# A fused attention and mixture-of-experts kernel: four groups of instructions are put elsewhere in the written order

## The chip, the cores and the metric

One core of a Trainium2 chip runs the whole program in one launch. The metric is the device time of one execution in microseconds (us). The kernel before takes 757.58 us, the median of 3 runs (757.49 to 758.53).

## The reference

Three layers follow each other in float32.

```python
# 1. attention, 4 batches x 8 heads, 576 positions, 64 dims; heads 0-3 see the last 32 positions,
#    heads 4-7 see the earlier positions that are congruent mod 32
attn = softmax(where(mask, q @ k.T / 8, -1e9)); x = (attn @ v) as [2304, 512]
# 2. dense layer, 512 -> 2048 -> 512
x = (s * relu(x @ w_in) ** 2 + b) @ w_out
# 3. experts: each token goes to one of 8 experts with room for 288 each, given out greedily by falling logit
logits = x @ w_gate
for (token, e) in argsort(-logits.flatten()):
    if token is free and counts[e] < 288: assigned[token] = e
out[assigned == e] = relu(x[assigned == e] @ w1[e]) @ w2[e]
```

## The kernel before

The order of all instructions is written by hand (a manual schedule): each engine executes its own instructions in the order in which the Python code emits them. The work is cut into generators, each `yield` ending one step; a `Pipe` (L46) starts a generator every so many ticks, and one `tick` advances all that are live by one step, oldest first.

Every float32 product is made of three: an operand is split into a high half (a cast on ScalarE, the engine ACT) and a low half (a subtraction on VectorE, DVE), and high x high, high x low and low x high are accumulated.

Attention (`attn_unit`, L234) has 32 units; one starts every second tick. A unit loads, makes scores (L254), takes a softmax on DVE and ACT, turns the weights by PE transposes (L292, L294), copies them, and multiplies with v (L313). For batches 0 and 1 the scores fall on even ticks and the transposes on odd ones (2 and 9 ticks after the start); for batches 2 and 3 (2 and 10 ticks) both fall on even ticks, and the older unit's transposes are emitted ahead of the newer one's scores.

`prep` (L372) decodes w_in and w_out. A slice of w_out is written to DRAM (L400), added into the column sums `acc` (L402, L404), and folded with the gate. `prep_end` (L456) multiplies `acc` with a matrix of ones and scales it by b (L459, L460). `load_out` (L449) reads the slices of w_out back later and splits them.

`mix1` (L565) interleaves attention, the first product (`h_step`, L469, 96 steps of 12 matmuls) and the preparation. The second product, x2, is done late: for each of 6 token groups and 16 slices `late_step` (L649) loads the activations r (L652), makes the high half u (L664) and the low half (L667), and puts 9 matmuls in a queue; each of these steps is one tick of `late_pipe`. `x2_late` (L685) hands the queued matmuls (L694) out one by one, and ticks the pipe when the queue is empty. After the last matmuls of a group come three calls of `x2_row` (L526), which combine an accumulator with `acc` on DVE (L530) and write 128 rows to DRAM from SP's queue (L531).

These matmuls fill PE while DVE decides the routing. `run` (L1045) takes a number from each `yield` of `route` (L740) and hands out that many x2 matmuls ("fill") before `route` goes on. A round of routing (7 in all, L805) picks each token's best open expert (`pick`, L801; L808 to L811) and finds each expert's threshold in four steps of 6 bits: a comparison with 64 candidates on DVE (L818, L820), a fill of FA0 (20) or FA (12), counting matmuls (L824), three small operations (L826 to L828), a fill of FB (7), and a matmul that spreads the result (L830). Then come T1, G1 and gsb (L831 to L834), a fill of FP (8), prefix sums (L726), a fill of FC (8), and the change of the assignment (L838 to L844), which runs straight into the next round's pick and first comparison. At the end FE gives the fills 4, 14 and 10. Every third yield `prep2` (L877) advances the loading and splitting of the first expert's weights (L367, L369).

Of the kernel before, what the change touches and what calls it, by code (L numbers as in the profile page):

```python
# [9 lines left out]
F32R = mybir.dt.float32r  # L10
# [64 lines left out]
class Body:  # L75
# [10 lines left out]
    E = 8  # L86
# [2 lines left out]
    WS = 68  # L89
    CA = 4  # L90
    LATE0 = 30
    FA0 = 20
    FA = 12
    FB = 7
    FP = 8
    FC = 8
    UB = 4
# [1 line left out]
    P1S = 28  # L99
    A2S = 8  # L100
    TM = 2
    FE = (4, 14, 10)
    P0S = 24
    AE = 2
    LOADLAG = 2
# [128 lines left out]
    def attn_unit(self, b, hp, hf):  # L234
# [51 lines left out]
        nc.vector.tensor_tensor(  # L286
            E[:pr], E[:pr], sm.unsqueeze(2).to_broadcast([pr, nb, kw]), op=ALU.mult)
        yield from self.lag(2, b)
        tps = [self.ps() for _ in range(2 if loc else 1)]
        for c in range(nb if loc else 4):  # L290
            if loc:
                nc.tensor.transpose(tps[c % 2][:96, 128 * (c // 2):128 * (c // 2) + 128], E[:, c, :], self.identf)  # L292
            else:
                nc.tensor.transpose(tps[0][:, 128 * c:128 * c + pr], Ep[:pr, 2 * c:2 * c + 2, :].rearrange("p m k -> p (m k)"),  # L294
                                    self.identf[:pr, :pr])
        yield
        eTs = []
        for t, tp in enumerate(tps):
# [20 lines left out]
        else:  # L319
            dst = self.xb[b][:, hp, :].rearrange("d (i m c) -> d m c i", m=2, c=8)[:, :, 4 * hf:4 * hf + 4]  # L320
            for m in range(2):
                (nc.vector.tensor_copy if m and self.OV else nc.scalar.copy)(
                    dst[:, m], o[m][:, :144].rearrange("d (c i) -> d c i", c=4))
        self.units += 1

    def keep_warm(self, n):
        if n:
# [44 lines left out]
    def prep(self, i):  # L372

        nc = self.nc
        fc = i // 2
        raw = self.conv_load(i)
        for _ in range(self.CA):
            yield
        rv = [t.rearrange("p (f t) -> p f t", t=2) for t in raw]
        K = self.wt([128, 512], I32, "K")  # L380
        ts = nc.vector.tensor_scalar
        half = (slice(0, 256), slice(256, 512))
        for r, h in zip(rv, half):
# [12 lines left out]
        yield  # L396
        if i % 2 == 0:
            yield from self.split(W, lambda v: self.win.__setitem__(fc, v))
            return
        nc.sync.dma_start(self.wod[fc], W)  # L400
        if fc == 0:
            nc.scalar.copy(self.acc, W)  # L402
        else:
            nc.vector.tensor_tensor(self.acc, self.acc, W, op=ALU.add)  # L404
        yield
        yield
        ps = self.ps()
        for dc in range(4):
            nc.tensor.transpose(ps[:, dc * 128:(dc + 1) * 128], W[:, dc * 128:(dc + 1) * 128], self.identf)  # L409
        yield  # L410
        WT = self.wt([128, 512], F32, "WT")
        nc.scalar.copy(WT, ps)
        yield
        self.WTs.append(WT)
        if len(self.WTs) < 4:
# [12 lines left out]
        ps = self.ps()  # L428
        for k in range(4):
            nc.tensor.transpose(ps[:, k * 128:(k + 1) * 128], go[:, k * 128:(k + 1) * 128], self.identf)  # L430
        yield
        nc.vector.tensor_reduce(self.wog[:, fc * 8 - 24:fc * 8 + 8].rearrange("p (f e) -> p f e", e=8),
                                ps.rearrange("p (f c e) -> p f e c", f=4, c=4)[:, :, :8, :], axis=AX.X, op=ALU.add)
        yield
        self.nwog += 4
        if self.nwog == 16:
            self.prep_end()

    def prep_begin(self):
        self.win, self.wout, self.xb, self.xg = {}, {}, {}, {}  # L440
        self.wod = self.dr.tile([16, 128, 512], F32, name="wod")
        self.nwog = self.units = self.ne = 0
        self.acc = self.c.tile([128, 512], F32, name="acc")
        self.wog = self.c.tile([128, 16 * 8 + 24], F32, name="wog")
        self.gate = self.c.tile([128, 4, 32], F32, name="gate")
        self.WTs = []
        self.sb = self.c.tile([128, 2], F32, name="sb")

    def load_out(self, fc):  # L449
        t = self.wt([128, 512], F32, "wo")  # L450
        self.nc.sync.dma_start(t, self.wod[fc])
        yield
        yield
        yield from self.split(t, lambda v: self.wout.__setitem__(fc, v))

    def prep_end(self):  # L456
        nc = self.nc
        ps = self.ps()
        nc.tensor.matmul(ps, self.onesf, self.acc, start=True, stop=True)  # L459
        nc.scalar.activation(self.acc, ps, AF.Copy, scale=self.sb[:, 1:2])  # L460
        ps = self.ps()
        nc.tensor.matmul(ps[:, :128], self.onesf, self.wog[:, :128], start=True, stop=True)
        lc = self.c.tile([128, 8], F32, name="lc")
        nc.vector.tensor_reduce(lc, ps[:, :128].rearrange("p (f e) -> p e f", e=8), axis=AX.X, op=ALU.add)
        nc.vector.tensor_scalar(lc, lc, self.sb[:, 1:2], None, op0=ALU.mult)
        self.lc = lc
# [52 lines left out]

    def x2_list(self, fc, acc, u, t=0):  # L520
        wh, wl = self.wout[fc]
        return [dict(out=acc[t + k], lhsT=u[:, j, k * 128:(k + 1) * 128], rhs=_alt(w),
                     start=(fc == 0 and i == 0), stop=(fc == 15 and i == 2))
                for k in range(u.shape[2] // 128) for i, (j, w) in enumerate(((0, wh), (0, wl), (1, wh)))]

    def x2_row(self, g, t, acc):  # L526
        nc = self.nc
# [37 lines left out]
    def mix1(self):  # L565
        nc = self.nc
        self.prep_begin()
        att, att2 = (Pipe(self.attention(*b), self.AE) for b in ((0, 1), (2, 3)))
        att.tick(self.AE)
        self.constants()  # L570
        self.L = self.c.tile([128, 18, 8], F32, name="L")
        self.R = self.c.tile([128, 18, 8], F32, name="R")
# [19 lines left out]
        ready = [(8, 0, dc) for dc in range(4)] + [(10, 1, 2), (11, 1, 0), (13, 1, 3), (14, 1, 1)]  # L592
        k = self.AE
        while self.units < 14 or not self.win or ready:
            att.tick()
            if k == self.SL:
                self.small_loads()
                nc.vector.memset(self.wog, 0.0)
                nc.gpsimd.iota(self.R, pattern=[[0, 18], [1, 8]], base=1, channel_multiplier=0,
                               allow_small_or_imprecise_dtypes=True)  # L600
            while ready and self.units >= ready[0][0]:
                self.group_x(*ready.pop(0)[1:])
            if self.KS <= k < self.KE:
                self.keep_warm(self.KW)
            if k >= self.P0S and k % self.P0R == 0:
                prep.tick()
            k += 1
# [3 lines left out]
        while True:  # L611
# [6 lines left out]
                if len(self.win) <= fc:  # L618
                    continue
            if self.units < 16:  # L620
                att.tick()
            elif n >= self.A2S:
                att2.tick()
            if n >= self.FS:
                for _ in range(self.FT):
                    if folds.started < len(order) and order[folds.started][1] >= self.nwog:
# [1 line left out]
                    folds.tick()  # L628
            if n >= self.WL and (n % 2 == 0 or n >= 84) and (lout.started < self.nwog or lout.started == 16):
                lout.tick()  # L630
            if n >= 95 and self.late_pipe.t < 5:
                self.late_pipe.tick()
            if fc == 12 and 0 < g < 5:
                need = 8 * (((g + 2) * self.G - 1) // self.S + 1)
                while self.units < need:
                    (att if self.units < 16 else att2).tick()
            if n == self.RC:
                self.route_consts()
            if n >= 96:
# [9 lines left out]
    def late_step(self, g, fc):  # L649
# [4 lines left out]
        yield  # L654
        last = g == self.last_late
        nt = 2 if last else 3
        u = self.p2.tile([128, 2, self.G], F32R, tag="u", name=self.nm("u"), bufs=self.UB)[:, :, :nt * 128]
        parts = [(u, r[:, :nt * 128])]
        if last:
            n = ("xh", "xl")[fc % 2]  # L660
            ul = self.xs.tile([128, self.G], F32R, tag=n, name=self.nm("ul"))[:, :256].rearrange("p (j t) -> p j t", j=2)
            parts.append((ul, r[:, 256:]))
        for d, src in parts:
            nc.scalar.copy(d[:, 0, :], src)  # L664
        yield
        for d, src in parts:
            nc.vector.tensor_tensor(d[:, 1, :], src, _f(d[:, 0, :]), op=ALU.subtract)  # L667
        yield
        if fc == 0:
            self.xacc[g] = self.x2_begin()  # L670
# [69 lines left out]
    def route(self):  # L740
# [64 lines left out]
        for rnd in range(7):  # L805
# [36 lines left out]
            tt(R, R, A1, op=ALU.mult)  # L842
            if rnd:
                tt(open_, open_, left, op=ALU.mult)  # L844
        pick()
        self.Rt, self.qt = R, q
        yield self.FE[0]
# [301 lines left out]
```

## Time and profile before

| | |
|---|---|
| time, median of 3 runs | 757.58 us |
| profiled execution, own time | 758.38 us |
| its span, first to last instruction | 756.5 us |
| PE (TensorE matmuls) busy | 731.5 us, 97% |
| PEld (weight loads) busy | 651.9 us, 86% |
| DVE, ACT busy | 497.5 us, 374.6 us |
| mean granted TensorE clock | 0.993 |

The profiled execution is one run with the hardware profiler. "Busy" counts the stretches covered by an instruction; matmuls are pipelined, so that one's end lies behind the next one's start, and the ends are modelled. Time not covered is the engine's idle time, and the profile names the instruction that ended it. By time the program has the attention start (0 to 55 us), the mix of attention and first product (to 315 us), the x2 product with the routing (to 526 us) and the experts.

### The profile page before, as it was taken

The page shows a single profiled execution, that of the slowest core. Times are in us where ns is not written, and L with a number is a line of the kernel's source. Part 1 is how long each engine was busy: PE and PEld are TensorE (multiplying, and loading weights), DVE is VectorE, ACT ScalarE, POOL GpSimd, SP SyncE. Part 2 cuts the span into 40 slices and gives each one's busy share as a digit, 9 for nine tenths or more (in the row PEclk, how much of TensorE's full clock was granted, in tenths as well). Part 3 has the DMA queues.
Part 4 walks back from the last instruction along what each step waited for, and adds up shares of the span by engine and source line. Part 5 has one row for each costly group of instructions (what it writes and reads, how often), then busy time and mean ns, then how long its engine had stood idle before and what let it go on. Part 6 is the DMA issues. An engine that isn't in the chain of part 4 may idle for free.

```text
span 756.5 us, 16924 instructions
## 1 busy us (share of the span) xinstructions
PE 731.5 (97%) x6436; PEld 651.9 (86%) x6436; DVE 497.5 (66%) x1229; ACT 374.6 (50%) x893; POOL 51.7 (7%) x69
## 2 busy tenths in 40 slices
PE   7979999999999999999989999999999999999996
PEld 5759999999999888787768887878999999999994
DVE  8789999898762133377777878687366666656620
ACT  3788776667766556422222232231355555555520
POOL 1000000000000000000000000000303221221211
PEclk9999999999999999999999999999999999999998
DMA  7885955774885799644325343342677668667411
GB/s 182 230 272 175 295 183 179 232 248 160 286 304 196 225 287 303 199 144 138 141 83 184 122 137 105 102 139 81 194 242 228 177 188 249 213 166 225 136 32 31
DMA packets 88752, 140.19 MB, mean 185 GB/s; under 512 B 10848, under 2 KB 52576, under 8 KB 88672
## 3 DMA queue, kind: packets, MB, share of 16 engines
q1 hardware_dynamic: 85600, 129.68, 54.5%
q0 software_dynamic: 3072, 9.44, 3.9%
q8 instruction: 50, 0.82, 0.5%
q14 instruction: 30, 0.25, 0.1%
HBM read 106.32 MB, written 32.77 MB: 184 GB/s over the span
## 4 chain that ended last, share of the span: by engine, by line
PE 88%; DVE 5%; DMA 4%; issue 1%; ACT 1%; SPq 0%; POOLq 0%; DVEq 0%; ACTq 0%
PE b L476 25%; PE b L694 19%; PE b L952 12%; PE b L977 11%; PE b L254 3%; DMA qk<-in_q_dram 2%; PE b L313 2%; PE b L513 2%; DMA r<-ud 1%; PE b L1015 1%; PE b L906 1%; DVE E L530 1%; PE b L993 1%; PE b L330 1%; PE b L409 1%
## 5 line engine op out<-in xcount | busy, mean ns | idle before, releaser
L694 PE MATMUL b<-wh,u 128*128 128x512 f32 x544 | 170.7, 390 | 5.5 <-DVE u L667 5.5
L694 PEld LDWEIGHTS b<-wh,u 128*128 128x128 f32 x544 | 101.5, 191 | 21.1 <-DVE u L667 7.7
L664 ACT CAST u<-r 128x384 fp32r<-128x384 f32 (+1 forms) x96 | 47.1, 493 | 141.2 <-PE b L694 102.2
L694 PE MATMUL b<-wl,u 128*128 128x512 f32 x272 | 105.6, 388 | 0.0
L977 PE MATMUL b<-u,wh 128*128 128x288 f32 x448 | 87.9, 293 | 0.0
L476 PE MATMUL b<-xh,wh 128*128 128x384 f32 x384 | 83.3, 340 | 0.0
L369 DVE TENSOR_TENSOR wl<-raw,wh 128x512 fp32r<-128x512 f32 x128 | 82.9, 683 | 0.4
L481 ACT ACTIVATE r<-b 128x384 f32<-128x384 f32 x96 | 47.0, 489 | 64.4 <-PE b L476 63.1
L476 PE MATMUL b<-xh,wl 128*128 128x384 f32 x384 | 78.9, 328 | 0.0
L476 PE MATMUL b<-xl,wh 128*128 128x384 f32 x384 | 78.8, 328 | 0.0
L367 ACT CAST wh<-raw 128x512 fp32r<-128x512 f32 x128 | 73.2, 618 | 1.5 <-DVE u L667 1.5
L952 PE MATMUL b<-X,wh 128*128 128x288 f32 x512 | 73.4, 286 | 0.6 <-ACT X L925 0.6
L476 PEld LDWEIGHTS b<-xh,wh 128*128 128x128 f32 x384 | 62.8, 190 | 8.6 <-issue 3.8
L977 PEld LDWEIGHTS b<-u,wh 128*128 128x128 f32 x448 | 69.4, 189 | 0.0
L952 PEld LDWEIGHTS b<-X,wh 128*128 128x128 f32 x512 | 67.4, 189 | 1.3 <-ACT X L925 0.7
L959 DVE SCALAR_TENSOR_TENSOR u<-b,u 128x288 fp32r<-128x288 f32 x64 | 29.2, 455 | 57.9 <-ACT u L958 43.8
L476 PEld LDWEIGHTS b<-xh,wl 128*128 128x128 f32 x384 | 65.5, 191 | 0.3 <-DVE wl L369 0.3
L476 PEld LDWEIGHTS b<-xl,wh 128*128 128x128 f32 x384 | 65.6, 191 | 0.0
L977 PE MATMUL b<-u,wl 128*128 128x288 f32 x224 | 64.1, 286 | 0.0
L694 PEld LDWEIGHTS b<-wl,u 128*128 128x128 f32 x272 | 51.8, 191 | 6.3
L667 DVE TENSOR_TENSOR u<-r,u 128x384 fp32r<-128x384 f32 (+1 forms) x96 | 49.1, 529 | 12.4 <-ACT u L664 12.3
L482 ACT ACTIVATE r<-r 128x384 f32<-128x384 f32 x96 | 50.5, 526 | 3.0
(211 smaller groups left out, 1113.5 us busy)
## 6 DMA issues: line engine op xcount, KB each, us to landing
raw<-in_moe_w_dram SPq DMA_DIRECT2D x128, 256.0 KB
r<-ud SPq DMA_DIRECT2D x160, 192.0 KB
ud<-r SPq DMA_DIRECT2D x96, 192.0 KB
raw<-in_words_dram SPq DMA_DIRECT2D x64, 256.0 KB
qk<-in_q_dram SPq DMA_DIRECT2D x24, 288.0 KB
x2d<-E SPq DMA_DIRECT2D x18, 256.0 KB
wod<-K SPq DMA_DIRECT2D x16, 256.0 KB
wo<-wod SPq DMA_DIRECT2D x16, 256.0 KB
```

The costliest lines, as they stand in the source:

```text
L254: nc.tensor.matmul(sp[64 * j:64 * j + p, c * kw:(c + 1) * kw], qk[sl, 0, q0:q0 + p], qk[sl, 1, k0:k0 + kw], start=after, stop=after or c = ...
L367: nc.scalar.copy(h, W)
L369: nc.vector.tensor_tensor(l, W, _f(h), op=ALU.subtract)
L476: nc.tensor.matmul(ps[:, :self.G], w[:, dc * 128:(dc + 1) * 128], _alt(self.xg[g][dc][x]), start=(k == 0), stop=(k == 11))
L481: nc.scalar.activation(_two(r), _nat(ps[:, :self.G]), AF.Relu)
L482: nc.scalar.activation(r, r, AF.Square)
L664: nc.scalar.copy(d[:, 0, :], src)
L667: nc.vector.tensor_tensor(d[:, 1, :], src, _f(d[:, 0, :]), op=ALU.subtract)
L694: self.nc.tensor.matmul(**args)
L952: self.nc.tensor.matmul(ps[:, :288], w1[dc, fh][wi][:, fs:fs + 128], _alt(X[:, xi, dc, :]), start=(k == 0), stop=(k == 11))
L959: self.nc.vector.scalar_tensor_tensor(_two(l), _nat(ps[:, :288]), 0.0, _two(_f(h)), op0=ALU.max, op1=ALU.subtract)
L977: nc.tensor.matmul(y[dc][:, :288], w[:, sl], _alt(u[:, j, :288]), start=(fc == 0 and i == 0), stop=(fc == 7 and i == 2))
```

## The change

Constants: FA0 20 to 13, FB 7 to 6, FE's third fill 10 to 20, and a new fill FK of 9 in rounds 0 to 5, between the change of the assignment and the next pick. In attention the transposes are collected while a tick runs and emitted at its end (`attend`). The column sums are taken from the slices that `load_out` reads back, and the product with ones follows the last of them. `late_step` waits one tick more between the low half and the matmuls; for groups 0 to 4 its halves are two tiles from a pool of 8 each, instead of one from a pool of 4.

```diff
-    FA0 = 20
+    FA0 = 13
+    FK = 9
-    FB = 7
+    FB = 6
-    FE = (4, 14, 10)
+    FE = (4, 14, 20)
...
-        tps = [self.ps() for _ in range(2 if loc else 1)]
-        for c in range(nb if loc else 4):
...
+        tps = []
+        def turn():
+            tps.extend(self.ps() for _ in range(2 if loc else 1))
+            for c in range(nb if loc else 4):
...
+        self.turns.append(turn)
         yield
...
+    def attend(self, pipe):
+        pipe.tick()
+        for turn in self.turns:
+            turn()
+        self.turns.clear()
...
         nc.sync.dma_start(self.wod[fc], W)
-        if fc == 0:
-            nc.scalar.copy(self.acc, W)
-        else:
-            nc.vector.tensor_tensor(self.acc, self.acc, W, op=ALU.add)
...
         yield from self.split(t, lambda v: self.wout.__setitem__(fc, v))
+        if fc == 0:
+            nc.scalar.copy(self.acc, t)
+        else:
+            nc.vector.tensor_tensor(self.acc, self.acc, t, op=ALU.add)
+        if fc == 15:
+            yield
+            yield
+            yield
+            ps = self.ps()
+            nc.tensor.matmul(ps, self.onesf, self.acc, start=True, stop=True)
+            nc.scalar.activation(self.acc, ps, AF.Copy, scale=self.sb[:, 1:2])
     def prep_end(self):
-        ps = self.ps()
-        nc.tensor.matmul(ps, self.onesf, self.acc, start=True, stop=True)
-        nc.scalar.activation(self.acc, ps, AF.Copy, scale=self.sb[:, 1:2])
...
-            if n >= 95 and self.late_pipe.t < 5:
+            if n >= 95 and self.late_pipe.t < 6:
...
-        u = self.p2.tile([128, 2, self.G], F32R, tag="u", name=self.nm("u"), bufs=self.UB)[:, :, :nt * 128]
+        if last:
+            u = self.p2.tile([128, 2, self.G], F32R, tag="u", name=self.nm("u"), bufs=self.UB)[:, :, :nt * 128]
+            u = u[:, 0], u[:, 1]
+        else:
+            u = [self.xs.tile([128, self.G], F32R, tag=n, name=self.nm("u")) for n in ("xh", "xl")]
...
         for d, src in parts:
-            nc.vector.tensor_tensor(d[:, 1, :], src, _f(d[:, 0, :]), op=ALU.subtract)
+            nc.vector.tensor_tensor(d[1], src, _f(d[0]), op=ALU.subtract)
+        yield
         yield
...
             tt(R, R, A1, op=ALU.mult)
             if rnd:
                 tt(open_, open_, left, op=ALU.mult)
+            if rnd < 6:
+                yield self.FK
         pick()
```

In `mix1` each tick of the attention pipes becomes a call of `attend`.

## Rows read from the trace of the kernel before

**Rows 1.** Busy time of each engine in stretches; then clock, DMA share, GB/s.
```profile
50.00:55.00 5.00, 2.47 (x36) 1.72 (x32) 4.79 (x15) 4.44 (x15) 0.00 (x0) 1.00 0.74 244
55.00:60.00 5.00, 5.00 (x33) 4.93 (x30) 4.93 (x14) 3.90 (x11) 0.00 (x0) 0.66 0.01 3
...
100.00:150.00 50.00, 50.00 (x635) 45.61 (x634) 45.58 (x110) 33.19 (x81) 0.00 (x0) 1.00 0.60 191
...
350.00:400.00 50.00, 45.43 (x289) 36.33 (x288) 36.75 (x92) 12.64 (x25) 0.00 (x0) 0.97 0.46 155
```
**Rows 2.** PE's waits, whole span: us in total, times, longest.
```profile
PE b L694 <- DVE u L667: 5.5, 4, 3.4
...
PE b L313 <- ACT eT L302: 1.8, 2, 0.9
PE b L292 <- DVE E L286: 0.8, 1, 0.8
...
PE b L830 <- DVE jc L828: 0.5, 1, 0.5
PE b L870 <- DVE rt L865: 0.3, 1, 0.3
PE b L824 <- DVE rt L820: 0.3, 1, 0.3
```
**Rows 3.** The chain of waits, 340 to 400 us: start, us, what.
```profile
381.27 1.61 PE b L694 x7
...
393.08 3.54 PE b L694 x9
...
396.87 1.85 PE b L694 x7
```
**Rows 4.** PE in order of time: start, duration, operation [idle before <-releaser].
```profile
371.76 0.39 PE L824 MATMUL b<-rt 128*128 128x16 bf16 x9
...
373.61 0.18 PE L830 MATMUL b<-J,unit 128*128 128x1 bf16 x1
...
385.36 0.46 PE L694 MATMUL b<-wl,u 128*128 128x512 f32 x1
...
389.33 0.38 PE L694 MATMUL b<-wl,u 128*128 128x512 f32 x1
393.08 0.70 PE L694 MATMUL b<-wh,u 128*128 128x512 f32 x2 [3.37 <-DVE u L667]
```
**Rows 5.** DVE in order of time, the same stage.
```profile
360.34 0.17 DVE L838 TENSOR_SCALAR rt<-b 128x8 f32<-128x8 f32 x1 [0.40 <-PE b L736]
...
361.78 0.30 DVE L802 TENSOR_REDUCE rt<-R 128x18 f32<-128x144 f32 x1
...
363.49 1.36 DVE L818 TENSOR_TENSOR rt<-rt,cand 128x1152 bf16<-128x1152 f32 x1
364.76 1.49 DVE L667 TENSOR_TENSOR u<-r,u 128x384 fp32r<-128x384 f32 x3
...
372.67 0.08 DVE L828 DVE_READ_ACCUMULATOR jc<-jo 64x1 bf16 x1
373.84 1.42 DVE L820 SCALAR_TENSOR_TENSOR rt<-rt,b,cand 128x1152 bf16<-128x1152 f32 x1 [1.09 <-PE b L830]
...
386.08 1.41 DVE L530 SCALAR_TENSOR_TENSOR E<-b,sb,acc 128x512 f32<-128x512 f32 x2 [1.48 <-PE b L694]
```
**Rows 6.** By line: the operations on the column sums.
```profile
L404 DVE TENSOR_TENSOR acc<-acc,K x15: 674/685/696, 152.1 to 231.8; 128x512 f32<-128x512 f32 x15
L460 ACT ACTIVATE acc<-b,sb x1: 687/687/687, 251.9 to 251.9; 128x512 f32<-128x512 f32 x1
```
**Rows 7.** ACT in order of time, at the start of the x2 product.
```profile
314.14 1.32 ACT L664 CAST u<-r 128x384 fp32r<-128x384 f32 x3
```
**Rows 8.** Waits of DVE, whole span, and of SP's queue, 313 to 526 us.
```profile
DVE u L667 <- ACT u L664: 12.3, 2, 11.9
...
SPq L531 <- DVE E L530: 97.2, 13, 23.6
```

More of the change, by code (lines that the diff above doesn't have):

```diff
@@ L288, in attn_unit @@
         yield from self.lag(2, b)
-        tps = [self.ps() for _ in range(2 if loc else 1)]
-        for c in range(nb if loc else 4):
-            if loc:
-                nc.tensor.transpose(tps[c % 2][:96, 128 * (c // 2):128 * (c // 2) + 128], E[:, c, :], self.identf)
-            else:
-                nc.tensor.transpose(tps[0][:, 128 * c:128 * c + pr], Ep[:pr, 2 * c:2 * c + 2, :].rearrange("p m k -> p (m k)"),
-                                    self.identf[:pr, :pr])
+        tps = []
+        def turn():
+            tps.extend(self.ps() for _ in range(2 if loc else 1))
+            for c in range(nb if loc else 4):
+                if loc:
+                    nc.tensor.transpose(tps[c % 2][:96, 128 * (c // 2):128 * (c // 2) + 128], E[:, c, :], self.identf)
+                else:
+                    nc.tensor.transpose(tps[0][:, 128 * c:128 * c + pr],
+                                        Ep[:pr, 2 * c:2 * c + 2, :].rearrange("p m k -> p (m k)"), self.identf[:pr, :pr])
+        self.turns.append(turn)
         yield
@@ L400, in prep @@
         nc.sync.dma_start(self.wod[fc], W)
-        if fc == 0:
-            nc.scalar.copy(self.acc, W)
-        else:
-            nc.vector.tensor_tensor(self.acc, self.acc, W, op=ALU.add)
         yield
@@ L440, in prep_begin @@
         self.win, self.wout, self.xb, self.xg = {}, {}, {}, {}
+        self.turns = []
         self.wod = self.dr.tile([16, 128, 512], F32, name="wod")
@@ L449, in load_out @@
     def load_out(self, fc):
+        nc = self.nc
         t = self.wt([128, 512], F32, "wo")
-        self.nc.sync.dma_start(t, self.wod[fc])
+        nc.sync.dma_start(t, self.wod[fc])
         yield
@@ L521, in x2_list @@
         wh, wl = self.wout[fc]
-        return [dict(out=acc[t + k], lhsT=u[:, j, k * 128:(k + 1) * 128], rhs=_alt(w),
+        return [dict(out=acc[t + k], lhsT=u[j][:, k * 128:(k + 1) * 128], rhs=_alt(w),
                      start=(fc == 0 and i == 0), stop=(fc == 15 and i == 2))
-                for k in range(u.shape[2] // 128) for i, (j, w) in enumerate(((0, wh), (0, wl), (1, wh)))]
+                for k in range(u[0].shape[1] // 128) for i, (j, w) in enumerate(((0, wh), (0, wl), (1, wh)))]
     def x2_row(self, g, t, acc):
@@ L568, in mix1 @@
         att, att2 = (Pipe(self.attention(*b), self.AE) for b in ((0, 1), (2, 3)))
-        att.tick(self.AE)
+        for _ in range(self.AE):
+            self.attend(att)
         self.constants()
@@ L594, in mix1 @@
         while self.units < 14 or not self.win or ready:
-            att.tick()
+            self.attend(att)
             if k == self.SL:
@@ L620, in mix1 @@
             if self.units < 16:
-                att.tick()
+                self.attend(att)
             elif n >= self.A2S:
-                att2.tick()
+                self.attend(att2)
             if n >= self.FS:
@@ L635, in mix1 @@
                 while self.units < need:
-                    (att if self.units < 16 else att2).tick()
+                    self.attend(att if self.units < 16 else att2)
             if n == self.RC:
@@ L656, in late_step @@
         nt = 2 if last else 3
-        u = self.p2.tile([128, 2, self.G], F32R, tag="u", name=self.nm("u"), bufs=self.UB)[:, :, :nt * 128]
+        if last:
+            u = self.p2.tile([128, 2, self.G], F32R, tag="u", name=self.nm("u"), bufs=self.UB)[:, :, :nt * 128]
+            u = u[:, 0], u[:, 1]
+        else:
+            u = [self.xs.tile([128, self.G], F32R, tag=n, name=self.nm("u")) for n in ("xh", "xl")]
         parts = [(u, r[:, :nt * 128])]
@@ L660, in late_step @@
             n = ("xh", "xl")[fc % 2]
-            ul = self.xs.tile([128, self.G], F32R, tag=n, name=self.nm("ul"))[:, :256].rearrange("p (j t) -> p j t", j=2)
+            ul = self.xs.tile([128, self.G], F32R, tag=n, name=self.nm("ul"))
+            ul = ul[:, :128], ul[:, 128:256]
             parts.append((ul, r[:, 256:]))
         for d, src in parts:
-            nc.scalar.copy(d[:, 0, :], src)
+            nc.scalar.copy(d[0], src)
         yield
         for d, src in parts:
-            nc.vector.tensor_tensor(d[:, 1, :], src, _f(d[:, 0, :]), op=ALU.subtract)
+            nc.vector.tensor_tensor(d[1], src, _f(d[0]), op=ALU.subtract)
+        yield
         yield
```

## The prediction

> **What bounds the kernel now.** I read the busy time by stretches first, then PE's waits, then the order of time on PE and DVE where PE waits longest. PE is the bound: from 100 to 150 us it has no idle time, though DVE is 91% busy and ACT 66% beside it [rows 1]. An edit can then only give back time in which PE waits or runs slowly. That time lies in two places. One is the end of the first half of attention (50 to 55 us, PE busy 2.47 of 5 us [rows 1]). The other is the x2 product with the routing (315 to 526 us), where 350 to 400 us alone has 4.57 us idle at a mean clock of 0.97 [rows 1].
>
> In the second place PE waits 5.5 us, four times, for a low half (L667), and 0.5, 0.3 and 0.3 us for the routing's own operations [rows 2]. The longest wait shows how. DVE runs a round's change of the assignment straight into the next pick and first comparison: start at 360.34, pick at 361.78, comparison at 363.49, and only then, at 364.76, three low halves [rows 5]. That is 4.4 us without a low half, while a low half is emitted one tick, 9 matmuls, ahead of its own matmuls. In the next round two calls of x2_row stood ahead of the same chunk (386.08, 1.41 us [rows 5]) and a third behind it; PE ran out at 389.5 and waited 3.37 us [rows 4]. The chain then has 9 matmuls in 3.54 us and 7 in 1.85, where 7 take 1.61 otherwise [rows 3]: the granted clock had fallen to the lower of its two levels, 1.2 instead of 2.4 GHz.
>
> At one point a rule of the notes says more. The Trainium skill ("Trainium Kernel Development and Optimization", Performance Expectations) holds matmul busy time for a poor measure, since matmuls are pipelined, and weight-load busy time for a good one. By weight loads 350 to 400 us is only 36.33 of 50 us busy [rows 1], so 13.7 us would be free instead of 4.57, and up to 9 us more could be won there. The fill itself says no: 19 of its matmuls start between 385.36 and 389.33 [rows 4], 0.22 us apart, against 0.213 us for 512 columns at 2.4 GHz. I go by PE's idle time.
>
> **Part by part.** *Transposes behind scores: 0.* For batches 0 and 1 the two never share a tick, so PE's order stays. For batches 2 and 3 it is reversed, in a stretch where PE has no idle time [rows 1] and waits for neither a softmax nor a weight copy: all such waits of the trace (1.8 and 0.8 us [rows 2]) are those of 50 to 55 us, before that half starts. What is queued behind scores that wait for a load would now include the transposes. Bounds: -0.3 to +0.5 us. It follows that the first place stays as it is.
>
> *Column sums: +0.2.* 15 additions of 0.685 us [rows 6], 10.3 us of DVE, leave 152 to 232 us and come after the slices are read back (241 to 303 us), where DVE waits for loads. PE is busy in both, so neither end counts. The product with ones and its scaling (0.687 us on ACT [rows 6]) move from 251 us to the step before the first x2 matmul. There ACT makes the first high halves at 314.14 [rows 7], directly ahead of PE's need at 314.9. With 0.7 us more in its queue and some 0.9 us more of PE ahead, ACT comes about 1.1 us later against 0.9 for PE. Between 0 and 0.7, I take 0.2.
>
> *The low halves' extra tick, 8 buffers, the split round: -5.5, and the clock -1.8.* The tick puts 18 matmuls (4.0 us) instead of 9 between a low half and its use. The fill of 9 lets one through between the pieces of 1.44 us (360.34 to 361.78) and 1.71 + 1.36 = 3.07 us [rows 5]. Neither piece reaches 4.0 us, so the four waits of 5.5 us go. With the 3.4 us gap the slow stretch after it goes: 3.54 - 9 x 0.23 = 1.5, and 1.85 - 1.61 = 0.24, in all about 1.8 us [rows 3]. The larger pool lets ACT make high halves sooner; DVE waits for one only twice in the whole trace, 11.9 of 12.3 us in one wait ahead of the first of them [rows 8], so 0 for that.
>
> *FA0 20 to 13, FB 7 to 6, FK 9: +3.7, -1.1.* A round has 13 + 3 x 12 + 4 x 6 + 8 + 8 + 9 = 98 matmuls instead of 100. From the prefix sums to the counting matmuls there are now 8 + 9 + 13 = 30, 6.6 us. DVE needs 0.24 + 1.44 + 0.5 (one low half) + 3.07 = 5.25 us; 1.35 us are spare. From the counting matmuls (371.76 [rows 4]) DVE's three operations are done at 372.75 [rows 5], and L830 followed at 373.61 [rows 4]; one matmul less leaves 0.6 of the 0.86 us. An ordinary round has no wait.
>
> Rounds with rows of x2 do. One row is 0.7 us on DVE and cannot start before PE has made its accumulator. The rows lie behind matmuls 138, 141 and 144 of each group's 144. The mix hands out 13 x 3 = 39, the fills before round 0 are 30 + 4 + 3 + 12 = 49, so round r starts at 88 + 98r, with the parts of a round at 13, 19, 31, 37, 49, 55, 67, 73, 81, 89 and 98. (Before, 39 + 49 + 700 + 28 = 816, all that the queue has.)
>
> - Group 0: 50, 53, 56 of round 0, behind counting work: 0.
> - Group 1: 96 of round 1 falls between the pieces, the other two behind the comparison. The row waits for PE until 3.5 us after the prefix sums and ends at 4.2; plus 3.07 is 7.3 against 6.6: 0.7 us. Then two rows, a low half and the three operations (1.4 + 0.5 + 0.56) end at 9.7, where L830 was due at 7.3 + 0.25 + 6 x 0.22 = 8.9: 0.8 us.
> - Group 2: 44, 47, 50 of round 3: two rows behind one comparison, one ahead of the next with an L369: 0.3 us.
> - Group 3: all three at 90, 93, 96 of round 4. They end at 4.3, a low half at 4.8, plus 3.07 is 7.85 against 6.6: 1.2 us.
> - Group 4: 38, 41, 44 of round 6, behind a comparison that ends at 1.65: with 2.1 of rows, 0.6 of low halves and 0.56, done at 4.85 where L830 was due at 4.2: 0.65 us.
>
> Together 0.7 + 0.8 + 0.3 + 1.2 + 0.65, some 3.7 us. Lower bound 0.5, if rows start earlier than their accumulators suggest; upper bound 6, if each of the six changes costs another 0.4. Before, rows fell elsewhere and cost, beside the waits for low halves, the 0.5 and 0.3 us that go now.
>
> SP's queue: a write of rows waits there for DVE (97.2 us in 13 waits [rows 8]), and the loads of r stand behind it. The extra tick emits one more load ahead of it. From load to low half is as before, three ticks, 27 matmuls or 6 us: 0.
>
> *FE 10 to 20:* 34 fills instead of 24 cover DVE's chain ahead of L870, so its 0.3 us go. Handed out in the route are 39 + 49 + 6 x 98 + 89 + 38 = 803; the last 13 run after L870, ahead of the 48 matmuls that cover the first gather. The last row is as much later as those 48: 0.
>
> **The sum.** Removed 5.5 + 1.8 + 0.5 + 0.3 + 0.3 = 8.4; new 3.7 + 0.2 = 3.9; net -4.5 us. The profiled execution took 758.38 us, 756.5 of span and 1.9 around it, and would take 753.9. The median is 0.8 lower, so 753.1 us. The forecast's own range is 751.1 to 754.6.
>
> **Rivals.** *All waits go:* DVE reaches the rows with time to spare, as the spare 1.35 us of ordinary rounds and 13 us of DVE idle in 350 to 400 us [rows 1] speak for. Against it: rows block everything queued behind them. 757.6 - 8.2 = about 749.6 us.
>
> *The lower clock stays:* group 1 has two waits 2 us apart, 1.5 us together, group 3 one of 1.2. At 50 to 55 us waits of at most 0.9 us each sufficed: PE was busy 2.47 of 5 us and the clock of 55 to 60 us is 0.66 [rows 1]. Against it: 1.5 us is less than 2.53. Price 1.8 us, once or twice: 754.9 to 756.7 us. The Trainium skill ("TensorE: Matmul & The Clock Gate", Why this matters for your kernels) asks that PE have no long gaps between bursts; by it short separate waits would cost no clock and 753.1 would stand, but the stretch from 50 to 60 us differs.
>
> *The waits only change their name:* the row, not the low half, holds DVE, and PE stands at L824 or L830 for as long as before. 757.6 - 1 to + 1: about 757 us.
>
> *Slower:* the 13 matmuls ahead of L824 (2.9 us) are fewer than its piece of DVE takes (3.07). If DVE comes late to the change in every round, behind low halves that wait for r behind SP's queue, the fill of 9 is no cover. It decides once DVE is 1.35 us late; at 2.8 us late, six rounds cost 6 x 1.45 = 8.7 us, above the 8.4 removed, and with one slow stretch the time is about 759.5 us. Against it: behind the first low half, DVE is held by a high half for 0.4 us in all [rows 8].
>
> **How the numbers follow.** The forecast has 0.50, all waits gone 0.13, the lower clock 0.14, renamed waits 0.13, slower 0.10. A change within 0.2% (1.5 us) is about what a measurement of this kernel can't tell from none. The clock rival lies on the faster side almost wholly, the renamed one on no change. Faster 0.76, same 0.14, slower 0.10. The range of 749.4 to 757.0 leaves out the slower case, half of the renamed waits and a small end of the best case.
>
> **What would show it.** After: no wait of PE for L667 above 1 us, the clock at 1.00 throughout 315 to 526 us, and PE's waits there at L824 and L830 next to rows of x2, some 3.9 us in all. 50 to 60 us as before. Another long wait for a low half, waits at L824 in rounds without rows, or a gain in the attention stretch would make the working wrong.

## The result and the profile after

The changed kernel takes 751.53 us, the median of 4 runs (750.04 to 752.22). Before, on the same chip, it was 757.54 us (757.26 to 758.53, 4 runs). The ratio is 0.9916, with a 95% interval of 0.9896 to 0.9935: 0.8% faster, inside the range of 749.4 to 757.0 and 1.6 us below the forecast of 753.1. The profiled execution took 752.19 us, 749.8 of span.

The stretches of [rows 1], in the changed kernel (us; busy time of PE, PEld, DVE, ACT, POOL; clock, DMA share, GB/s):

```profile
50.00:55.00 5.00, 4.20 (x42) 3.42 (x43) 4.86 (x15) 4.36 (x14) 0.00 (x0) 0.54 0.31 116
55.00:60.00 5.00, 5.00 (x28) 4.78 (x28) 4.86 (x14) 4.11 (x13) 0.00 (x0) 0.77 0.00 0
100.00:150.00 50.00, 48.63 (x652) 45.29 (x651) 46.11 (x111) 33.74 (x80) 0.00 (x0) 1.00 0.62 200
350.00:400.00 50.00, 48.83 (x328) 39.82 (x325) 40.13 (x105) 17.28 (x35) 0.00 (x0) 1.00 0.57 190
```

From 350 to 400 us PE has 1.17 us idle, where it had 4.57, and its clock is full. That was forecast. From 100 to 150 us PE now has 1.37 us idle, where it had none. That was not. The difference at 50 to 55 us is not the change's: a second profile of the kernel before has PE busy for 4.42 us there, at a clock of 0.50.

PE's waits in the changed kernel, whole span (us in total, times, longest), the answer to [rows 2]:

```profile
PE b L849 <- DVE rt L843: 1.6, 2, 1.1
...
PE b L719 <- DVE u L691: 1.1, 1, 1.1
PE b L494 <- DVE wl L381: 1.1, 1, 1.1
PE b L855 <- DVE jc L853: 0.9, 2, 0.6
...
PE b L319 <- DVE eT L308: 0.3, 1, 0.3
```

L849 and L855 are the counting and spreading matmuls (L824 and L830 before), L719 and L691 are x2 and its low half (L694, L667), L494 is the first product (L476), L319 the products with v (L313). The low halves' 5.5 us in four waits are now 1.1 in one. In the x2 stage all waits above 0.25 us sum to 6.5 us before and 3.6 after. Two waits in the attention are new against that profile, 1.1 us for the low half of a weight and 0.3 for softmax weights. The first is not new in kind: two further profiles of the kernel before have 0.58 and 0.39 us at the same place.

Where the time went, by starts of the same matmul in each profile. "Attention" is from the first of the first product (L476, after L494) to the first of its 47th step; "x2" from the first of x2 to the first for the last 128 rows (L906, after L933). Both kernels and the one with the transposes alone were profiled again for this:

| profile | own time | attention | x2 | clock low in x2 |
|---|---|---|---|---|
| before | 758.38 | 130.05 | 210.53 | 393.8 us, for 3.4 |
| before_2 | 757.52 | 130.10 | 210.56 | 392.1 us, for 3.4 |
| before_3 | 757.21 | 129.99 | 210.60 | 392.3 us, for 3.4 |
| t_only | 754.24 | 128.53 | 208.93 | never |
| t_only_2 | 753.31 | 128.17 | 208.87 | never |
| after | 752.19 | 128.24 | 206.82 | 514.7 us, for 3.4 |
| after_2 | 750.26 | 128.50 | 205.12 | never |

The experts repeat: from the first matmul of L952 (after L979) to the last it is 197.2 us in every profile. Attention gives back 1.5 to 1.9 us, x2 3.7 or 5.4.

### The profile page after: what moved, and what is told of

Read it like the earlier page. It is cut to its first block, busy times and chain, and to the rows that moved or that the text cites. A ratio compares the mean times of both kernels' runs of the same rounds, so it can differ in the third digit from the quotient of the medians.

```text
span 749.8 us, 16912 instructions
## 1 busy us (share of the span) xinstructions
PE 728.5 (97%) x6436; PEld 651.5 (87%) x6436; DVE 497.0 (66%) x1229; ACT 374.8 (50%) x893; POOL 52.4 (7%) x69
## 4 chain that ended last, share of the span: by engine, by line
PE 85%; DVE 10%; ACT 2%; issue 1%; DMA 1%; SPq 0%; POOLq 0%; DVEq 0%
PE b L719 22%; PE b L494 21%; PE b L979 13%; PE b L1004 11%; PE b L531 2%; PE b L255 2%; PE b L319 2%; PE b L1042 1%; PE b L933 1%; PE b L1020 1%; PE b L342 1%; DVE W L402 1%; PE b L417 1%; PE b L967 1%; PE b L296 1%
## 5 line engine op out<-in xcount | busy, mean ns | idle before, releaser
L719 PE MATMUL b<-wh,u 128*128 128x512 f32 x544 | 169.8, 389 | 1.1 <-DVE u L691 1.1
L719 PEld LDWEIGHTS b<-wh,u 128*128 128x128 f32 x544 | 101.6, 191 | 15.2 <-DVE u L691 1.8
L688 ACT CAST u<-r 128x384 fp32r<-128x384 f32 (+1 forms) x96 | 46.4, 493 | 129.3 <-DMA r<-ud 64.7
L719 PE MATMUL b<-wl,u 128*128 128x512 f32 x272 | 105.7, 389 | 0.0
L494 PE MATMUL b<-xh,wh 128*128 128x384 f32 x384 | 83.6, 341 | 0.0
L494 PE MATMUL b<-xh,wl 128*128 128x384 f32 x384 | 78.3, 327 | 1.1 <-DVE wl L381 1.1
L494 PE MATMUL b<-xl,wh 128*128 128x384 f32 x384 | 78.8, 328 | 0.0
L979 PE MATMUL b<-X,wh 128*128 128x288 f32 x512 | 73.4, 286 | 0.6 <-ACT X L952 0.6
L494 PEld LDWEIGHTS b<-xh,wh 128*128 128x128 f32 x384 | 63.0, 191 | 7.4 <-PE b L531 3.1
L979 PEld LDWEIGHTS b<-X,wh 128*128 128x128 f32 x512 | 67.4, 189 | 1.3 <-ACT X L952 0.7
L494 PEld LDWEIGHTS b<-xh,wl 128*128 128x128 f32 x384 | 65.2, 190 | 1.4 <-DVE wl L381 1.4
L494 PEld LDWEIGHTS b<-xl,wh 128*128 128x128 f32 x384 | 65.6, 191 | 0.0
L691 DVE TENSOR_TENSOR u<-r,u 128x384 fp32r<-128x384 f32 (+1 forms) x96 | 49.3, 529 | 16.5 <-ACT u L688 16.2
L719 PEld LDWEIGHTS b<-wl,u 128*128 128x128 f32 x272 | 51.9, 191 | 6.4
```

Of the source, the lines that this page charges most:

```text
L494: nc.tensor.matmul(ps[:, :self.G], w[:, dc * 128:(dc + 1) * 128], _alt(self.xg[g][dc][x]), start=(k == 0), stop=(k == 11))
L688: nc.scalar.copy(d[0], src)
L691: nc.vector.tensor_tensor(d[1], src, _f(d[0]), op=ALU.subtract)
L719: self.nc.tensor.matmul(**args)
L979: self.nc.tensor.matmul(ps[:, :288], w1[dc, fh][wi][:, fs:fs + 128], _alt(X[:, xi, dc, :]), start=(k == 0), stop=(k == 11))
```

## Experiments

### The changed kernel with the transposes where they were: t_inplace

```diff
-        self.turns.append(turn)
+        turn()
```

> The changed kernel, with the transposes emitted where they stood before (older unit's transposes ahead of the newer unit's scores); all else changed. Switch theory: PE loses about 0.12 us when it goes from the products on 36, 64 or 96 rows to a full-array instruction and about 0.15 us on the way back, inside what counts as busy; undoing the order costs 0.27 us in each of 12 shared ticks and about 2.4 to 3.2 us in all: 751.5 becomes 754 to 754.7. Rival, the prediction's own term: no effect where PE has no idle time, 751.5 within 0.5, and the 3 us that the first 315 us got shorter are run-to-run spread of the start.

Measured: 752.42 us (751.5 to 754.28), ratio 0.9929 [0.9915, 0.9942]. Neither number holds: it lies between the two. The total hides what the trace shows. One tick with all three kinds of small products, PE in order of time (start, us, operation), first before, then after, then t_inplace:

```profile
108.78 0.67 PE L313 MATMUL b<-eT,v 36*64 36x36 f32 x32
109.39 0.75 PE L292 MATMUL b<-identf,E 128*96 128x128 f32 x5
110.07 0.88 PE L254 MATMUL b<-qk 64*64 64x96 f32 x16
110.88 0.92 PE L476 MATMUL b<-xh,wh 128*128 128x384 f32 x4
```
```profile
106.66 0.67 PE L319 MATMUL b<-eT,v 36*64 36x36 f32 x32
107.15 0.87 PE L255 MATMUL b<-qk 64*64 64x96 f32 x16
107.95 0.75 PE L296 MATMUL b<-identf,E 128*96 128x128 f32 x5
108.46 0.90 PE L494 MATMUL b<-xh,wh 128*128 128x384 f32 x4
```
```profile
107.37 0.67 PE L319 MATMUL b<-eT,v 36*64 36x36 f32 x32
107.97 0.75 PE L296 MATMUL b<-identf,E 128*96 128x128 f32 x5
108.66 0.88 PE L255 MATMUL b<-qk 64*64 64x96 f32 x16
109.46 0.92 PE L494 MATMUL b<-xh,wh 128*128 128x384 f32 x4
```

From the first product with v to the first matmul of the next step is 2.10 us before (110.88 - 108.78), 1.80 after and 2.09 with the old order. No idle time stands in any of these rows. The rows name the part of the array in use, rows * columns: 36*64 for these products with v, 64*64 for scores, 128*96 (or 100*128) for transposes, 128*128 for the first product. The median step from the start of the last matmul of one kind to the start of the first of the next, in ns: v to transposes 153, transposes to scores 179 (100-row transposes) or 202 (128-row), scores to the first product 172 (129 where scores use 36 columns). In the new order: v to scores 39, scores to transposes 173 (130), transposes to the first product 28. Two dear steps per tick become cheap ones, and one stays.

There are 11 ticks with all three kinds. In five of them the products with v next to the scores use 96*64, and their step to the scores is 152 ns: there only the step from transposes to the first product is cheap. Such a tick gets 0.15 to 0.18 us shorter (one of the five can't be read, as it now has a wait of 0.30 us inside), the other six 0.27 to 0.30. From the last matmul of the step before to the first of the step behind, less PE's waits, the 11 ticks sum to 26.2 us before and in t_inplace, and 23.9 after and in t_only: 2.3 us, the same to 0.02 us in every profile of these. That is 0.21 us per tick, where the expectation had 0.27. In the one tick with scores and transposes but no v product nothing changes (1.28 us in all).

The total is only 0.9 us above the changed kernel's: in the profiles, PE's wait for DVE in the attention is 0.56 us here instead of 1.07 and 0.3, and the clock stayed full in x2, which the changed kernel's did in one profile of two.

### Transposes ahead of everything in the tick: t_first

```diff
-        yield from self.lag(2, b)
+        for _ in range((self.LAG if b > 1 else self.LAG0)[2] - 1):
+            yield
...
         self.turns.append(turn)
+        yield
...
     def attend(self, pipe):
-        pipe.tick()
         for turn in self.turns:
             turn()
         self.turns.clear()
+        pipe.tick()
```

> The changed kernel, with the transposes emitted at the start of the tick, ahead of the older unit's products with v and of the newer unit's scores. Switch theory: the order full-array, products with v, scores has as many switches as the changed order (full-array work of the h steps stands on both sides), so the time is that of the changed kernel, 751.5 within 0.7. Rival: what counts is that scores start earlier, or that the softmax has more time before the transposes; then it costs what the old order does, 754 to 754.7.

Measured: 752.57 us (751.29 to 753.76), ratio 0.9929 [0.9915, 0.9943], 0.4 us above the switch theory's range and 1.4 below the rival's. The same tick, PE in order of time:

```profile
106.50 0.71 PE L297 MATMUL b<-identf,E 128*96 128x128 f32 x5
107.14 0.67 PE L321 MATMUL b<-eT,v 36*64 36x36 f32 x32
107.63 0.87 PE L255 MATMUL b<-qk 64*64 64x96 f32 x16
108.43 0.92 PE L496 MATMUL b<-xh,wh 128*128 128x384 f32 x4
```

Its 11 ticks take 23.9 us too, with a wait of 1.28 us at 122.9 us. Being behind the scores is not what pays. In both orders the transposes stand next to the first product, and v and scores stand side by side. In the profile the clock fell to its lower level at 514.4 us for 3.4 us, as in the one called after.

### The transposes alone, in the kernel before: t_only

```diff
-                nc.tensor.transpose(...)
+        def turn():
+            ...
+        self.turns.append(turn)
...
-            att.tick()
+            self.attend(att)
```

> The kernel before with the transposes behind the scores and nothing else. Switch theory: each of 12 shared ticks is 0.27 us shorter on PE, part of it lost again to a wait for DVE near 122 us, so 1.3 to 2.6 us less than before (757.5 to 758.0 here): a ratio of 0.9966 to 0.9983, and the route with the waits for low halves of before, 3.4 us the longest. Rival, the prediction's term: ratio 0.9993 to 1.0007.

Measured: 753.99 us (753.68 to 754.77), ratio 0.9954 [0.9941, 0.9967]: 3.4 us, more than either theory gave. Attention gives 1.5 to 1.9 us of it: 2.3 from the ticks, and back go 0.7 to 1.0, as PE has two waits for DVE of 1.1 and 0.2 to 0.3 where each profile of the kernel before has one wait (0.33 us for a load, or 0.58 and 0.39 for DVE). Another 0.1 to 0.5 us, by which profiles are paired, no row here accounts for. The other 1.7 us lie in x2 (210.56 to 208.9), where every wait is as before, the 3.37 us too. To see whether that is chance, both kernels were profiled again.

### The same kernels profiled again: before_2, before_3, t_only_2, after_2

> The kernel before, unchanged, profiled a second time. Theory A: where the clock falls is decided by PE's waits, so the lower clock stands behind the 3.37 us wait at about 393 us again (3.4 us long), the first one at about 56 us is 3.4 us long again, and every stage between the two agrees within 0.1 us. Theory B: the lower clock differs from execution to execution with the same program; the waits are the same to 0.1 us, but the stretch behind the 3.37 us wait or the one near 50 us has another length, and the time to the first h matmul differs by up to 1 us.

> The kernel before, unchanged, a third profile: as for the second. Three profiles of one program give the spread of its stages: by theory A below 0.3 us in each, by theory B up to 1.7 us in the x2 stage and up to 1 us ahead of the first h matmul.

> The kernel before with the transposes behind scores alone, profiled a second time. Theory A: no lower clock behind its 3.37 us wait, as the first time, so the x2 stage up to the tail's product takes 208.9 us again, and the later place of that wait is what saves it. Theory B: it is chance, and the stage takes 208.9 or 210.5 us. By both, from the 16th to the 47th block of h takes 93.7 us and DVE's wait at 124 us is 1.1 us.

> The changed kernel, unchanged, profiled a second time. Theory A: the 1.10 us wait for the last low half at 512 us is followed by 3.4 us at the lower clock again, and the x2 stage up to the tail's product takes 206.8 us. Theory B: that stretch comes and goes, and without it the stage takes 205.1 us with the same seven waits.

Six microseconds around the 3.37 us wait, columns as in the first view (PE busy first, clock third from the end), then PE's first matmuls behind it; before_2, then t_only_2:

```profile
391.00:397.00 6.00, 4.97 (x23) 3.97 (x24) 3.00 (x9) 1.46 (x3) 0.00 (x0) 0.72 0.70 220
```
```profile
392.03 1.21 PE L694 MATMUL b<-wh,u 128*128 128x512 f32 x2 [3.36 <-DVE u L667]
...
393.45 1.06 PE L694 MATMUL b<-wh,u 128*128 128x512 f32 x2
```
```profile
388.80:394.80 6.00, 5.03 (x31) 4.12 (x32) 3.85 (x10) 1.45 (x3) 0.00 (x0) 1.00 0.73 228
```
```profile
389.77 0.70 PE L707 MATMUL b<-wh,u 128*128 128x512 f32 x2 [3.37 <-DVE u L680]
...
391.17 0.59 PE L707 MATMUL b<-wh,u 128*128 128x512 f32 x2
```

The same wait, the same matmuls: two take 1.06 us in the one and 0.59 in the other. The lower clock followed the wait in all three profiles of the kernel before and in neither of t_only. Theory A holds there for these two. Near 50 us theory B does, for the kernel before: the lower level lasted 3.4, 10.2 and 6.8 us in its three profiles, and the first product started up to 1.1 us earlier. In x2 theory B holds for the changed kernel: eight microseconds around its 1.1 us wait at 512, after and then after_2:

```profile
511.00:519.00 8.00, 7.10 (x53) 6.07 (x54) 3.05 (x9) 0.00 (x0) 0.00 (x0) 0.79 0.02 9
```
```profile
511.40:519.40 8.00, 7.11 (x61) 6.40 (x62) 4.16 (x11) 0.00 (x0) 0.00 (x0) 1.00 0.10 37
```

PE is busy for as long, and the clock is 0.79 in one and 1.00 in the other; that is the 1.7 us between 206.82 and 205.12. The other runs say the same. The wait of 1.10 us stands also in t_first, t_inplace, split_back and sums_back, and only in t_first did the clock fall behind it; in fa15 it is 1.75 us and the clock stayed full. So a wait's length alone does not decide the clock. That the place of the wait counts as well would fit, but is not shown: no run here moved a wait by itself, and three profiles against two leave room for chance in t_only. The Trainium skill ("TensorE: Matmul & The Clock Gate", Part 1) says that the gate's watching runs freely and does not start with the kernel.

### The round's change in one piece: split_back

```diff
-    FA0 = 13
-    FK = 9
+    FA0 = 22
...
-            if rnd < 6:
-                yield self.FK
```

> The changed kernel without the fill between the two pieces: FA0 22, no FK, the round still 98 matmuls, the extra tick of the low halves kept. Theory A (the extra tick alone removes the waits for low halves; a whole piece of 4.5 us is shorter than 18 matmuls and the three of the third product, 4.6 us; and rows of x2 of groups 1 and 3 then fall behind the comparison): the waits of 1.2 and 1.06 us next to rows go, 749.3 to 750.5. Theory B (the split is needed to let a low half through): waits for L691 come back, 2 us or more, and 753.5 to 756.

Measured: 751.69 us (751.42 to 751.88), ratio 0.9918 [0.9905, 0.9931]. Neither number holds. PE's waits in x2 are 0.71, 0.86, 0.53, 0.55, 0.34 and 1.10 us, 4.1 in all against 3.6. The waits for low halves that come back are one of 0.86 us (the 1.10 at the end was there), not one of 3.4, and PE's waits for the routing's own operations don't go.

### The low halves one step less ahead: lead_back

```diff
-            if n >= 95 and self.late_pipe.t < 6:
+            if n >= 95 and self.late_pipe.t < 5:
...
             nc.vector.tensor_tensor(d[1], src, _f(d[0]), op=ALU.subtract)
-        yield
         yield
```

> The changed kernel with the low halves one tick ahead again instead of two (the second wait step taken out); the pool of 8, the split round and the rest kept. Theory A, that either the tick or the split is enough: in an ordinary round the second piece ends 5.3 us after the prefix sums and the low half behind it at 5.8, while its first use is at 6.4, so no wait; next to rows of groups 1 and 3 and at the closing operations 0.4 to 1.7 us are added: 752 to 753.2. Theory B, the prediction's: the tick is what removes the waits; then waits for L691 of 3 us and more in all come back, with a stretch at the lower clock: 755 to 757.

Measured: 751.94 us (751.58 to 753.55), ratio 0.9933 [0.992, 0.9946]. Theory A's number holds within 0.1 us, theory B's does not. There are three waits for low halves, 0.86 us the longest, instead of four with 3.37. With either the step or the split the long waits are gone. Both runs kept the eight buffers, and no run takes those back. But buffers alone can't have ended the wait of 3.37 us: in the kernel before, DVE works from 386.08 to the low half at 392.48 us without a pause, on rows, the change, the pick and the comparison, and is held by a high half for 0.4 us in all behind the first [rows 8].

### The column sums where they were: sums_back

```diff
         nc.sync.dma_start(self.wod[fc], W)
+        if fc == 0:
+            nc.scalar.copy(self.acc, W)
+        else:
+            nc.vector.tensor_tensor(self.acc, self.acc, W, op=ALU.add)
...
     def prep_end(self):
         nc = self.nc
+        ps = self.ps()
+        nc.tensor.matmul(ps, self.onesf, self.acc, start=True, stop=True)
+        nc.scalar.activation(self.acc, ps, AF.Copy, scale=self.sb[:, 1:2])
```

> The changed kernel with the column sums taken in prep again and their product with ones in prep_end, as before. Theory: nothing of it is on the path; the time from the first product of the h steps to the first x2 matmul is that of the changed kernel within 0.3 us, and the total 751.5 within 0.7. Rival: the 10.3 us of DVE taken out of 145 to 232 us are part of what made the first 315 us shorter; then 752.3 to 753.5, and PE waits for DVE between 145 and 235 us.

Measured: 750.23 us (749.64 to 750.81), ratio 0.9906 [0.9892, 0.9921]. From the last matmul of the first product to the first of x2 it is 0.41 us as before, 0.49 in the changed kernel. The waits in x2 are the changed kernel's, 1.10 at 511.7 included, with the clock full behind it. What the move itself does is 0.1 us, as the theory had it. The median is 1.3 lower than the changed kernel's and 0.6 below the expected range, but the two ratios' intervals overlap. The clock that stayed full is worth 1.7 in one execution, and no run tells whether anything else is in it.

### A longer first fill: fa15

```diff
-    FA0 = 13
+    FA0 = 15
```

> The changed kernel with FA0 15 instead of 13, so that 14 more of the queue's matmuls are handed out before the routing ends and none is left behind it. Theory: the last wait for a low half (1.1 us) and the stretch at the lower clock after it (about 1.7 us) come from low halves of the last slices still standing behind DVE's closing operations; with the queue that far ahead both go (-2.8), and the two longer rounds next to rows of x2 wait less (-1 to -1.7): 747 to 748.7. Rival: the lower clock comes from the 36 small matmuls of the index product and not from the wait; then -1.1 to -2.8: 748.7 to 750.4. If FA0 does nothing but shift work: 751.5.

Measured: 750.19 us (749.82 to 752.56), ratio 0.9904 [0.989, 0.9918], a miss of 1.5 us and more. The number lies in the rival's range, but the rival is not shown: the 36 small matmuls run here too, and the clock stayed full. Waits beside rows are 0.40, 1.06 and 0.85 us, and the wait for the last low half grew to 1.75 at 514.1 us. Two matmuls more per round leave fewer for the end, but one low half still stood behind the closing operations.

### A better version: ends

```diff
-    FA0 = 13
+    FA0 = 15
-    FE = (4, 14, 20)
+    FE = (4, 16, 18)
...
+        if last and fc > 13:
+            u = self.wt([128, 512], F32R, "u")
+            u = u[:, :256], u[:, 256:]
-        if last:
+        elif last:
```

> FA0 15, FE 4, 16, 18, and the high and low halves of the last group's last two slices in tiles of another pool, so that all low halves stand ahead of the closing operations and DVE isn't held there by a high half that waits for a buffer. Theory: the wait of 1.1 us of the changed kernel (1.75 us with FA0 15) comes from DVE being held 1.4 to 1.5 us by the pool of 4 and from a low half emitted behind the closing operations; it shrinks to 0.5 us or less, and with FA0 15 the time is 748.5 to 750. Rival: the wait for the low half becomes one for the index operations (L892), of 1 us or more, and the time stays at 750.2.

Measured: 749.45 us (748.58 to 749.83), ratio 0.989 [0.9875, 0.9905]. The number is as expected. It is below the kernel before by 1.1%, and all four runs lie under the changed kernel's lowest (750.04), though the two ratios' intervals still touch. PE's waits (us, times, longest) name no low half of x2 any more, and no index operations either; L858 and L852 are the spreading and counting matmuls:

```profile
PE b L858 <- DVE jc L856: 1.2, 2, 0.8
PE b L852 <- DVE rt L846: 1.1, 1, 1.1
PE b L494 <- DVE wl L381: 1.0, 1, 1.0
```

The x2 stage takes 203.60 us, 1.5 less than after_2. Fills and buffers were changed together, so the run doesn't tell which did how much.

## Why the prediction was right, and where it failed

The sum was -4.5 us and the medians give -6.0.

**Transposes: 0 predicted, -1.6 measured.** This is the step that failed, and its bounds of -0.3 and +0.5 with it; a gain in the attention stretch was named as what would make the working wrong. The working said that a stretch without idle time has nothing to give [rows 1]. It has: 2.3 us of steps between products on different parts of the array stood inside PE's busy time, and the profile names no wait for them. The Trainium skill ("TensorEngine Tiling (Array Packing)", Tiling Modes, Key Properties) states that changing the tiling mode drains TensorE. No run here shows that these steps are such changes, but weighed against this edit that line would have spoken for a gain; the prediction did not weigh it. PEld's busy time did not show it either: 45.61 us of 50 before and 45.29 after.

What is late next was missed too. DVE was busy 45.58 of 50 us [rows 1], and PE, quicker by 2.3, runs into it. DVE in order of time, changed kernel, ahead of PE's 1.07 us wait, which ends at 123.12 us:

```profile
120.16 0.66 DVE L287 TENSOR_TENSOR E<-E,nm 128x480 f32<-128x480 f32 x1
120.74 0.55 DVE L269 TENSOR_TENSOR E<-b,mloc 128x384 f32<-128x384 f32 x1
121.32 0.55 DVE L271 TENSOR_REDUCE nm<-E 128x4 f32<-128x384 f32 x1
121.91 0.56 DVE L280 TENSOR_TENSOR E<-E,nm 128x384 f32<-128x384 f32 x1
122.38 1.29 DVE L381 TENSOR_TENSOR wl<-K,wh 128x512 fp32r<-128x512 f32 x2
```

DVE goes without a pause from softmax work to the low half that PE needs.

**Low halves: -5.5 predicted, and the four waits go.** The reason holds up to the closing operations: no piece of DVE's work keeps a low half from PE for long. But lead_back and split_back show that the 18 matmuls of lead were not needed beside the split.

**The clock: -1.8 predicted.** The slow stretch behind the 3.37 us wait is worth 1.7 us (210.56 less t_only's 208.9), as sized. That it goes with the wait is not the whole cause: t_only kept the wait and lost the stretch. Nor was the clock full throughout, as forecast: in the profile called after it fell at 514.7 us, and 1.7 us were lost again. That is the price of the rival in which the lower clock stays, but behind the last low half and not beside rows.

**New waits beside rows: +3.7 predicted, 2.5 measured.** Four of the five are where the groups were placed. DVE in order of time, group 1, changed kernel:

```profile
381.43 0.75 DVE L548 SCALAR_TENSOR_TENSOR E<-b,sb,acc 128x512 f32<-128x512 f32 x1 [1.33 <-PE b L719]
382.10 0.29 DVE L827 TENSOR_REDUCE rt<-R 128x18 f32<-128x144 f32 x1
...
383.79 1.36 DVE L843 TENSOR_TENSOR rt<-rt,cand 128x1152 bf16<-128x1152 f32 x1
385.07 1.40 DVE L548 SCALAR_TENSOR_TENSOR E<-b,sb,acc 128x512 f32<-128x512 f32 x2
386.39 0.55 DVE L691 TENSOR_TENSOR u<-r,u 128x384 fp32r<-128x384 f32 x1
386.97 0.17 DVE L851 COPY jo<-b 64x8 f32<-64x8 f32 x1
```

A row (L548) holds DVE for 1.33 us until PE has made its accumulator, the pick and the comparison follow, and PE waits 0.57 us at L849 (385.21); then two rows and a low half stand ahead of the small operations, and PE waits 0.59 at L855 (387.58). Predicted were 0.7 and 0.8. Group 3 has 1.06 us for 1.2, group 4 0.31 for 0.65, group 2 none for 0.3. So the rival in which every wait goes is out (its 757.6 - 8.2 is 749.4, not 749.6), and so are renamed waits of the old size and the slower case, by all four runs.

**The end: -0.3 predicted, +0.8 measured.** L870's wait went. But no wait for a low half was to be above 1 us, and one of 1.10 is. Unforeseen was that it stands behind the whole closing chain. DVE in order of time, changed kernel:

```profile
505.66 0.42 DVE L691 TENSOR_TENSOR u<-r,u 128x256 fp32r<-128x256 f32 x1 [1.51 <-ACT u L688]
506.00 0.28 DVE L691 TENSOR_TENSOR ul<-r,ul 128x128 fp32r<-128x128 f32 x1
506.20 0.30 DVE L877 TENSOR_TENSOR rt<-b,rt 128x144 f32<-128x144 f32 x1
...
510.91 0.60 DVE L892 TENSOR_TENSOR rt<-rt,iotat 128x432 bf16<-128x432 bf16 x1
```

From 506.20 to 511.4 DVE makes no low half, and PE waits for the next one:

```profile
510.42 0.38 PE L719 MATMUL b<-wl,u 128*128 128x512 f32 x1
511.90 0.70 PE L719 MATMUL b<-wh,u 128*128 128x512 f32 x2 [1.10 <-DVE u L691]
```

The last group still takes its halves from the pool of 4, which the prediction never followed. ACT waits there until PE has used a buffer:

```profile
505.22 0.40 ACT L688 CAST u<-r 128x256 fp32r<-128x256 f32 x1 [1.54 <-PE b L719]
```

So DVE is held 1.51 us for a high half (L688), and then the chain is first. With other buffers for the last two slices and the fills shifted, as in ends, the wait is gone.

**Column sums: +0.2 predicted, 0.1 measured.**

**What held, then.** Measured between before_2 and after_2: attention -1.6; x2 -5.4, of which waits are -2.9 (6.5 to 3.6) and the clock -1.7. The last 0.8 lie in x2's busy time, and no run here tells what they are. With the clock full, the parts make -7.0 where the sum had -4.5: the transposes missed by -1.6, the rows by -1.2, the end by +1.1, and -0.8 is not accounted for. In executions where the clock falls at 514 us, as in the profile called after, 1.7 are lost again. So the median of -6.0 came out nearer to the sum than the steps deserve, and that is luck.

The first 55 us were to stay, and no change beyond the spread of the same program shows: the first matmul of the first product starts at 55.50, 54.44 and 54.47 us in the three profiles of before, at 54.35 and 54.50 in the two of after.

## What to carry to other kernels

An engine that is busy throughout can still lose time inside its busy rows: compare start to start across each change of shape, and put products that use the same part of the array side by side. When an order gets quicker on one engine, name the engine that is next in that stretch and subtract its wait at once. For a producer that runs ahead, follow its buffers to the very last item, where the closing work stands in its queue.

## What the runs showed of the hardware

Steps between float32 matmuls, from the start of the last of one kind to the start of the first of the next, with the rows * columns of the array in use: 36*64 or 96*64 (v) to transposes (100 or 128 rows) 153 ns; transposes to 64*64 (scores) 179 to 202; 64*64 to transposes or to the first product (128*128) 172 to 173; 96*64 to 64*64 152; but 36*64 to 64*64 only 39, and transposes to the first product 28.

A wait of 3.37 us was followed by the clock's lower level in three profiles of one program and not in two of another; one of 1.1 us in one of two profiles of the changed kernel, in t_first, and not in t_inplace, split_back and sums_back. Around 50 us the lower level lasted 3.4, 6.8 or 10.2 us (before, after, t_only) with PE's program there the same in all; the start of the first product, 54.3 to 55.5 us in these, did not follow its length.
